# Sliding-window attention into a feed-forward layer: loads of the first blocks reordered and paired, the division of three blocks moved behind AV

## The chip, the cores and the metric

The kernel runs on one core of a Trainium2 chip. The metric is device microseconds of that core, the median of three runs. A profile is one execution, taken by the hardware profiler.

## The reference

```python
# q, k, v: (8, 8, 576, 64) f32; out: (4608, 512) f32
scores = q @ k.T / 8;  only |i - j| <= 32 is kept (others -1e9)
attn   = softmax(scores)                     # sum + 1e-9 below
x      = (attn @ v) as (4608 tokens, 512 = 8 heads x 64)
h      = x @ w_in                            # (512, 2048)
g      = s * relu(h)**2 + b                  # s, b: one number each
out    = g @ w_out                           # (2048, 512)
```

## The kernel before

The 4608 tokens are cut into 36 blocks of 128. For block j the attention needs 128 rows of q, and k and v from 32 rows before the block to 96 beyond, which lie in the tiles j and j+1 (k and v are loaded with an offset of 32 rows). The steps of one block are these:

- `load_k`, `load_q`, `load_v` (L456) put f32 tiles of 128 tokens into SBUF, by one DMA each (two where a tile spans two sequences). In HBM a token's 64 numbers of one head lie together: 256 bytes.
- `cast_k`, `cast_q`, `cast_v` make bf16 copies (`kqn`, `ve`); `make_vo` makes a second copy of v with its halves shifted (`vo`).
- `k_turn` (L546) and `q_turn` (L559) transpose k and q on TensorE for the first blocks (up to `KQDMA` = 8), with a copy out of PSUM (`kqt`); later blocks use a DMA transpose for k and q together (L539).
- `attend`: 16 or 24 small score matmuls (`sc`, L596), on VectorE the mask with the row minimum (L605), on ScalarE eight exponentials with row sums (L612, its accumulator is read by an extra instruction), on VectorE 1e-9 added and a reciprocal (L620, L623), then eight products p times 1/sum (L477; blocks 0 to 2 share them between ScalarE, VectorE and GpSimd, later blocks leave them to GpSimd), a transpose of p (TensorE for j below `PDMA` = 4, L646; else a DMA transpose, L639), AV matmuls (`av`, L667) and a copy into `xt` (bf16).

The feed-forward layer (FFN) works on tiles of 128 tokens (8 of them) and then 256 tokens (14). Its first layer (L758) multiplies `xt` by `win`, ScalarE takes the relu (L767), VectorE squares into `gt` (L786). The second layer (L809) accumulates 16 slices of `wout` in PSUM, four matmuls at a time; VectorE scales by s, adds `cvec` and writes `outs` (L818). `cvec` is b times the column sums of w_out, by matmuls of ones (L694) as the slices of w_out come in. The weights come in eight f32 DMAs of 1 MB (i0 to i3 for w_in, o0 to o3 for w_out; L431), staged in parts of `gt` that are not used yet, and are cast by three engines.

All work is listed first, as nodes with their reads, writes, an engine (or a choice of engines), a cost and a key. A planner (`order`) then simulates the five engines and SP's DMA ring and, on each engine, takes the ready node with the lowest key. The keys are token positions, shifted by kind of work through a table `RANK`. `akey(j)` gives attention's key, ahead of the FFN by up to `LEAD` tokens. TensorE nodes that use a part of its array have a mode other than 0; the planner charges a switch of modes and favours staying (`STICK`). Where it sees TensorE idle in the head, it puts in matmuls of ones that compute nothing (`fill`, L408). The loads are chained to each other on SP's queue; the first of them follow a written list:

```python
FIRST = "k0 k1 q0 v0 v1 k2 q1 v2 i0 i1 i2 k3 q2 v3 k4 q3 v4 i3 o0 o1 o2 o3|||"
PDMA, KQDMA, AHEAD, GATE = 4, 8, 4, 5
```

A `|` separates what is issued at the start from what is issued after block 0, 1, ... of attention has been listed. From then on, the loads of block j + `AHEAD` follow block j. The two scalars s and b (`scb`) are loaded on ScalarE's queue at the start.

Of the kernel before, what the change touches and what calls it, by code (L numbers as in the profile page):

```python
# [5 lines left out]
F32 = mybir.dt.float32  # L6
# [4 lines left out]
S = 576  # L11
# [12 lines left out]
START, RING, ISSUE, LAND, TURN = 800.0, 2400.0, 700.0, 2000.0, 600.0  # L24
PE_SLACK, STEADY = 400.0, 60000.0
SWITCH, STICK, STAY = 95.0, 1500, 60000.0
BIAS = {"act": 0.0, "dve": 400.0, "pool": 0.0}
FILL, FILL_MIN, FILL_SHARE, FILL_NS, WARM = ("attn", "ffn", "sums"), 300.0, 0.7, 115.0, 9000.0


class _Node:
# [4 lines left out]
                 "hard", "mode")  # L36

    def __init__(self, nid, eng, fn, cost, lat, key, dsem, ndma, dtime):
# [21 lines left out]
        self.mode = 0  # L60


class _Plan:
# [10 lines left out]
    def add(self, eng, fn, cost, key, reads=(), writes=(), dsem=None, ndma=1, dtime=0.0,  # L74
            after=(), behind=None, ndesc=128):
        n = _Node(len(self.nodes), eng, fn, cost, 300.0 if eng == "pe" else 130.0, key, dsem,
                  ndma, dtime)
        n.ndesc = ndesc

# [23 lines left out]
    def order(self):  # L103
# [14 lines left out]
        dma_free = {"sp": 0.0, "pool": 0.0, "act": 0.0}  # L118
# [14 lines left out]
        while len(out) < len(self.nodes):  # L133
# [29 lines left out]
            if e == "pe" and n.mode != mode:  # L163
                free[e], mode = free[e] + SWITCH, n.mode
            if n.dsem is None:
                end = free[e] + n.lat
            else:
                early = t < STEADY
                if e == "sp" and early:
                    free[e] = room(free[e], n.ndesc)  # L170
                dma_free[e] = max(dma_free[e], free[e] + (ISSUE if early else 1300.0)) + n.dtime
                if e == "sp" and early:
                    dma_free[e] += TURN if (n.ndesc == 512) != (kind == 512) else 0.0
                    kind = n.ndesc
                end = dma_free[e] + (LAND if early else 700.0)
                if e == "sp":
                    queue.append((dma_free[e], n.dtime, n.ndesc))
                    del queue[:-12]
            for u in n.users:
                if u.deps[n] is None:  # L180
                    u.ready = max(u.ready, free[e])
                else:
                    late = PE_SLACK if u.eng == "pe" and t > STEADY else 0.0
                    u.ready = max(u.ready,
                                  end + late if u.eng != n.eng or n.dsem else free[e] + 60.0)
                u.left -= 1
                if u.left == 0:
                    offer(u)
# [70 lines left out]
    stage = None  # L259


def bass_sliding_window_symmetric__then__act_starrelu_kernel(
# [15 lines left out]
    LEAD, L0, LS = 640, 300, 50  # L278
    RELU, SQ = 400, 200
    FIRST = "k0 k1 q0 v0 v1 k2 q1 v2 i0 i1 i2 k3 q2 v3 k4 q3 v4 i3 o0 o1 o2 o3|||"  # L280
# [3 lines left out]
    PDMA, KQDMA, AHEAD, GATE = 4, 8, 4, 5  # L284
# [5 lines left out]
    NSPLIT, NWHOLE, NSOLO = 0, 0, 0  # L290

    RANK = ({"ptc": 200, "ou": 120, "no": -20, "av": -120, "vo": 0, "ktc": 0, "ck": 200, "rc": -160, "cv": 20, "ktd": 320, "cq": 400, "wo": 340, "s1": -240, "kt": -60, "wi": -40, "xt": -280, "re": 80, "pt": -40}, {"vo": 40, "pt": -60, "ex": -200, "ck": -320, "s2": -80, "av": 580, "qt": -320, "mx": 320, "s1": -20, "sc": 40, "kt": 80})
    EARLY = 12

    def rank(kind, j):
        return RANK[0 if j < EARLY else 1].get(kind, 0)

# [15 lines left out]
    with ExitStack() as es:  # L313
# [10 lines left out]
        NL, NB, NVE, NVO, NKT, NP, NS, NPT, NG, NR1, NO, NM = 4, 4, 5, 4, 5, 4, 4, 3, 12, 4, 4, 4  # L324
# [4 lines left out]
        Q32 = [sb((128, DM), F32, "q32") for _ in range(NL)]  # L329
        K32 = [sb((128, DM), F32, "k32") for _ in range(NL + 1)]  # L330
# [18 lines left out]
        ONES = sb((128, 256), BF16, "ones")  # L349
        NIL = sb((128, 128), BF16, "nil")  # L350
# [8 lines left out]
        PTPF = ps((128, 512), F32, "ptp")  # L359
        AV = ps((128, NPAIR, 128), F32, "av")  # L360
# [13 lines left out]
        add("dve", lambda e: e.memset(NIL[:], 0.0), 100, K0, writes=["NIL"])  # L374
        add("dve", lambda e: e.memset(FLAT[:, 0, :], NEG), 100, K0, writes=[("FLAT", 0)])
        add("dve", lambda e: e.memset(FLAT[:, 1, :], 0.0), 100, K0, writes=[("FLAT", 1)])
        add("dve", lambda e: e.memset(K32[0][0:32, :], 0.0), 485, K0 + 10, writes=[("K32", 0, "lo")])
# [24 lines left out]
        def fill(e, stage, n):  # L402
            for _ in range(n):
# [3 lines left out]
                else:  # L407
# [8 lines left out]
        add("act", lambda e: [e.dma_start(SCB[:, 0:1], moe_s[0:1].partition_broadcast(128)),  # L416
                             e.dma_start(SCB[:, 1:2], moe_b[0:1].partition_broadcast(128))],
            900, K0, writes=["SCB"], dsem="dscb", ndma=2, dtime=400)
# [3 lines left out]
        wcnt = [0]  # L422

        def load_w(which, c):
            s_ = wcnt[0] % 4
# [4 lines left out]
                   else w_out[:, 4 * c:4 * c + 4, :])  # L430
            lastload[0] = add("sp", lambda e: [e.dma_start(w32, src)], 500, -LEAD - 900,  # L431
                              writes=[("W32", s_, g) for g in range(4)], dsem=f"dw{s_}",
                              dtime=2780, behind=lastload[0], ndesc=512)
# [18 lines left out]
        def load(src, t0, dst, name, key, sem, x):  # L452
            pcs = parts(t0)

            def fn(e):
                return [e.dma_start(dst[r:r + n, :].rearrange("p (h d) -> p h d", h=H),  # L456
                                    src[b, :, s0:s0 + n, :].rearrange("h s d -> s h d"))
                        for (b, s0, r, n) in pcs]

            tot = sum(n for (_, _, _, n) in pcs)  # L460
            gate = turned.get(x - GATE)
            lastload[0] = add("sp", fn, 640.0 * len(pcs), key, writes=[name], dsem=sem,
                              ndma=len(pcs), dtime=1150.0 * tot / 128, behind=lastload[0], ndesc=8 * tot,
                              after=[gate] if gate and gate.eng == "pe" else [])
# [3 lines left out]
        def cast(engs, src, sname, dst, dname, key, costs=None):  # L468
            move(engs, costs or {"act": 620.0, "dve": 425.0, "pool": 640.0}, dst, src, key,
                 sname if isinstance(sname, list) else [sname], [dname])  # L470

        def move(engs, costs, dst, src, key, reads, writes, scale=None):
# [12 lines left out]
            if isinstance(engs, str):  # L485
                return add(engs, fns[engs], costs[engs], key, reads=reads, writes=writes)
            return add(tuple(engs), fns, costs, key, reads=reads, writes=writes)

        def load_q(j):
            s_ = j % NL  # L490
            load(q, 128 * j, Q32[s_], ("Q32", s_), 128 * j - LEAD - 600, f"dq{s_}", j)

        def cast_q(j):
            s_, d_ = j % NL, (j + 1) % NB
# [3 lines left out]
        def load_k(j):  # L498
            s_ = j % (NL + 1)
            load(k, 128 * j - 32, K32[s_], ("K32", s_), 128 * j - LEAD - 730, f"dk{s_}", j - 1)  # L500

        def cast_k(j):
            s_, d_ = j % (NL + 1), j % NB
            cast(CSET(j), K32[s_][:, :], [("K32", s_)] + ([("K32", 0, "lo")] if j == 0 else []), KQN[d_][:, 0:DM],
# [12 lines left out]
        def make_vo(j):  # L517
# [9 lines left out]
            for r0, x in ((64, j), (0, j + 1)):  # L527
                sl = x % (NL + 1)
                move(OSET(j), {"act": 620.0, "dve": 425.0},
# [5 lines left out]
        def k_turn(j):  # L535
            kn, kt = j % NB, j % NKT
            key = akey(j) - 128
            if j > KQDMA:
                add("sp", lambda e: [e.dma_start_transpose(KQT[kt][:, :, :], KQN[kn][:, :])],  # L539
                    1300, key + 64 + rank("ktd", j), reads=[("KN", kn), ("QN", kn)],  # L540
                    writes=[("KT", kt), ("QT", kt)], dsem=f"dkt{kt}", dtime=1600, ndesc=1024)
# [8 lines left out]
            move(FLEX(j - 1), {"dve": 430.0, "act": 620.0}, KQT[kt][:, 0:NPAIR, :], TP[:, 0:4, :],  # L550
                 key + rank("ktc", j), ["TP"], [("KT", kt)])

        def q_turn(j):
            qn, qt = (j + 1) % NB, (j + 1) % NKT
            key = akey(j)

            def fn(e):
                for pr in range(NPAIR):
                    r = e.transpose(TP[:, 4 + pr, :],  # L559
                                    KQN[qn][:, DM + 128 * pr:DM + 128 * pr + 128], IDENT[:, :])  # L560
                return r

            if j >= KQDMA:
                return
            add("pe", fn, 240, key + rank("qt", j), reads=[("QN", qn), "IDENT"], writes=["TP"])
            move(FLEX(j), {"dve": 430.0, "act": 620.0}, KQT[qt][:, NPAIR:2 * NPAIR, :], TP[:, 4:8, :],
                 key + rank("qtc", j), ["TP"], [("QT", qt)])

        def attend(j):
# [7 lines left out]
            def half(blk, pr, a):  # L577
                return ((NKT - 1 - blk) * 2 * NPAIR + pr) * 2 + a

# [20 lines left out]
            add("pe", scores, 215, key + rank("sc", j), reads=[("KT", ka), ("KT", kb), ("QT", kb)],  # L600
# [284 lines left out]
```

## Time and profile before

| | |
|---|---|
| median of three runs | 322.82 us (322.29 to 323.59) |
| span of the profiled execution, first to last instruction | 322.6 us |
| TensorE busy | 309.6 us (96%), 3437 matmuls |
| ScalarE, VectorE, GpSimd busy | 237.1, 219.0, 188.1 us |
| HBM read, written | 36.70 MB, 9.44 MB |

No time is recorded for the profiled execution beside its span; the span lies within the three runs' range. Busy time of TensorE includes the matmuls of ones. A row of a timeline reads: start, duration (us), engine, line, operation, what it writes and reads, how many were merged, and in brackets the idle time before it with what ended it. A row of a table of windows reads: window, its length, then busy time and instruction count of PE, PEld, DVE, ACT and POOL, the granted clock, the busy share of the DMA engines and GB/s.

### The profile page before, as it was taken

The page shows a single profiled execution, that of the slowest core. Times are in us where ns is not written, and L with a number is a line of the kernel's source. Part 1 is how long each engine was busy: PE and PEld are TensorE (multiplying, and loading weights), DVE is VectorE, ACT ScalarE, POOL GpSimd, SP SyncE. Part 2 cuts the span into 40 slices and gives each one's busy share as a digit, 9 for nine tenths or more (in the row PEclk, how much of TensorE's full clock was granted, in tenths as well). Part 3 has the DMA queues.
Part 4 walks back from the last instruction along what each step waited for, and adds up shares of the span by engine and source line. Part 5 has one row for each costly group of instructions (what it writes and reads, how often), then busy time and mean ns, then how long its engine had stood idle before and what let it go on. Part 6 is the DMA issues. An engine that isn't in the chain of part 4 may idle for free.

```text
span 322.6 us, 9452 instructions
## 1 busy us (share of the span) xinstructions
PE 309.6 (96%) x3437; PEld 210.7 (65%) x3437; DVE 219.0 (68%) x939; ACT 237.1 (73%) x804; POOL 188.1 (58%) x402
## 2 busy tenths in 40 slices
PE   6879899998999999999999999999999999999996
PEld 4557675757775766566666766676766666766664
DVE  3657848976896678787677875678776766644242
ACT  4988977896995878797578986788889888624130
POOL 1555785886878275769565887467686754420000
PEclk9999999999999999999999999999999999999999
DMA  7999999999999999999999999999999992230011
GB/s 143 293 285 267 399 262 221 213 207 216 201 215 182 257 212 178 223 212 227 214 217 219 200 197 216 216 230 188 194 234 211 240 157 67 68 98 2 33 68 65
DMA packets 185887, 62.49 MB, mean 194 GB/s; under 512 B 177008, under 2 KB 177264, under 8 KB 185840
## 3 DMA queue, kind: packets, MB, share of 16 engines
q1 hardware_dynamic: 185552, 61.88, 94.6%
q8 instruction: 27, 0.44, 0.6%
q14 instruction: 20, 0.16, 0.2%
q10 hardware_dynamic: 288, 0.00, 0.0%
HBM read 36.70 MB, written 9.44 MB: 143 GB/s over the span
## 4 chain that ended last, share of the span: by engine, by line
PE 77%; SPq 8%; DMA 8%; POOL 3%; DVE 2%; ACT 1%; issue 1%; POOLq 0%
PE ht L758 24%; PE outp L809 15%; PE ptp L809 15%; PE tp L758 10%; SPq L456 7%; PE av L667 4%; DMA q<-in_q_dram 3%; PE sc L596 3%; PE sc L809 2%; DMA kqt<-kqn 2%; POOL p L477 2%; DMA v<-in_v_dram 2%; PE av L809 2%; DMA pts<-p 1%; PE outp L694 1%; SPq L431 1%
## 5 line engine op out<-in xcount | busy, mean ns | idle before, releaser
L477 POOL TENSOR_SCALAR p<-p,rc 128x128 bf16<-128x128 bf16 x275 | 112.7, 428 | 35.9 <-DVE rc L623 35.9
L612 ACT ACTIVATE p<-ss,mx 128x128 bf16<-128x128 f32 x288 | 111.8, 391 | 11.1 <-DVE mx L605 10.6
L758 PE MATMUL ht<-xt,win 128*128 128x256 bf16 (+1 forms) x1104 | 106.5, 248 | 0.2
L786 DVE TENSOR_TENSOR gt<-r 128x512 bf16<-128x512 bf16 x144 | 71.3, 497 | 48.2 <-ACT r L767 46.3
L758 PEld LDWEIGHTS ht<-xt,win 128*128 128x128 bf16 x1104 | 86.5, 98 | 18.2 <-ACT r L767 0.6
L767 ACT ACTIVATE r<-ht 128x512 bf16<-128x512 f32 x106 | 62.4, 591 | 31.2 <-PE ht L758 29.7
L605 DVE CUSTOM_DVE_ANT_0 ss<-sc,mask 128x128 f32<-128x128 f32 x288 | 66.2, 282 | 8.8 <-PE sc L596 8.5
L809 PE MATMUL outp<-wout,gt 128*128 128x512 bf16 (+1 forms) x272 | 67.8, 373 | 0.0
L809 PE MATMUL ptp<-wout,gt 128*128 128x512 bf16 x256 | 65.5, 379 | 0.0
L612 ACT ACTIVATION_READ_ACCUMULATOR p<-ss,mx 128x1 f32 x288 | 54.6, 189 | 0.0
L758 PE MATMUL tp<-xt,win 128*128 128x256 bf16 x304 | 39.4, 273 | 0.0
L809 PEld LDWEIGHTS ptp<-wout,gt 128*128 128x128 bf16 x256 | 24.2, 98 | 22.1
L809 PEld LDWEIGHTS outp<-wout,gt 128*128 128x128 bf16 x272 | 24.9, 98 | 20.1
L476 POOL CAST ve<-v 128x512 bf16<-128x512 f32 x37 | 24.1, 651 | 24.0 <-PE av L667 14.4
L481 ACT CAST vo<-v 64x512 bf16<-64x512 f32 x45 | 27.6, 614 | 12.0 <-PE av L667 10.3
L758 PEld LDWEIGHTS tp<-xt,win 128*128 128x128 bf16 x304 | 29.3, 98 | 7.5
L476 POOL CAST kqn<-k 128x512 bf16<-128x512 f32 x33 | 21.4, 648 | 20.8 <-DMA k<-in_k_dram 20.7
L767 ACT ACTIVATE r<-tp 128x512 bf16<-128x512 f32 x38 | 22.4, 590 | 14.6 <-PE tp L758 13.3
L476 DVE CAST xt<-av 128x512 bf16<-128x512 f32 (+1 forms) x34 | 23.1, 680 | 9.0 <-PE av L667 8.8
L476 POOL CAST kqn<-q 128x512 bf16<-128x512 f32 x34 | 22.5, 661 | 10.4 <-DMA q<-in_q_dram 10.3
L605 DVE DVE_READ_ACCUMULATOR2_ANT mx<- 128x1 f32 x288 | 23.0, 80 | 0.0
L596 PEld LDWEIGHTS sc<-kqt 64*64 64x64 bf16 x632 | 9.8, 106 | 12.5 <-issue 8.5
(69 smaller groups left out, 229.7 us busy)
## 6 DMA issues: line engine op xcount, KB each, us to landing
out_dram<-outs SPq DMA_DIRECT2D x35, 256.0 KB, 2.9
q<-in_q_dram SPq DMA_DIRECT2D x32, 256.0 KB, 4.7
k<-in_k_dram SPq DMA_DIRECT2D x28, 256.0 KB, 4.5
v<-in_v_dram SPq DMA_DIRECT2D x28, 256.0 KB, 4.8
gt<-in_moe_w_in_dram SPq DMA_DIRECT2D x4, 1024.0 KB, 8.3
gt<-in_moe_w_out_dram SPq DMA_DIRECT2D x4, 1024.0 KB, 9.3
k<-in_k_dram SPq DMA_DIRECT2D x8, 192.0 KB, 3.6
v<-in_v_dram SPq DMA_DIRECT2D x8, 192.0 KB, 4.3
```

The lines of the kernel that those rows point to most:

```text
L456: return [e.dma_start(dst[r:r + n, :].rearrange("p (h d) -> p h d", h=H), src[b, :, s0:s0 + n, :].rearrange("h s d -> s h d")) for (b, s0, ...
L476: return e.tensor_copy(dst, src)
L477: return e.tensor_scalar(dst, src, scale, 1.0, ALU.mult, ALU.mult)
L481: return e.copy(dst, src)
L596: r = e.matmul(dst, rhs=rhs, start=True, stop=True, lhsT=KQT[kb][r0:r0 + 64, NPAIR + pr, 64 * u:64 * u + 64])
L605: lambda e, ss=ss, x=x, y=y: e.tensor_tensor_reduce(out=SS[ss][:, x, :], in0=SC[y % 2][:, y // 2, :], in1=MASK[kind][:, :], scale=-SCALE, ...
L612: lambda e, ss=ss, x=x, y=y: e.activation(P[pb][:, y, :], SS[ss][:, x, :], AF.Exp, bias=MX[mb][:, y:y + 1], scale=-1.0, accum_out=SM[mb][: ...
L667: r = e.matmul(avp[64 * hh:64 * hh + 64, pr, 64 * u:64 * u + 64], lhsT=vt[k0:k1, 128 * pr + 64 * hh:128 * pr + 64 * hh + 64], rhs=PTS[ptb] ...
L758: r = e.matmul(hbank[:, nt * f:nt * f + nt], lhsT=WIN[:, kc, 128 * ft:128 * ft + 128], rhs=XT[:, kc, x0:x0 + nt], start=(kc == 0), stop=(k ...
L767: return e.activation(R1[rb][:, :], hbank[:, :], AF.Relu, bias=0.0, scale=1.0)
L786: return e.tensor_tensor(d, r, r, ALU.mult)
L809: r = e.matmul(op_[:, 0:cn], lhsT=GT[:, g_, fc, :], rhs=WOUT[:, fc, c0:c0 + cn], start=(fc == 0), stop=(fc == 15))
```

## The change

- The list of first loads is new. k and q of the first ten blocks come in pairs of blocks: `K0` is the k of blocks 0 and 1, and so on. One partition takes two neighbouring tokens, so that a run in HBM is 512 bytes. Tokens of four blocks come before the first weight; w_in is loaded in one piece, then v4 and K2, then w_out and, last, the scalars, now on SP's queue.
- The pairs are cast in two strided halves and turned together (`turn_pair`); the copy out of PSUM puts even and odd tokens back in order with a stride. `KQDMA` goes from 8 to 10, so k 9, k 10, q 8 and q 9 are turned on TensorE too.
- Blocks 0 to 2 (`NPN`) no longer multiply p by 1/sum: the exponentials take no row sums, matmuls of ones give the sums in `xt`'s layout (with 1e-9 from a constant tile `EPS`), VectorE takes the reciprocal (`RB`) and multiplies where it copied AV into `xt`.
- Blocks 0 and 1 (`NSPLIT`) do without `vo`: their AV takes three steps on `ve` of two tiles.
- `AHEAD` goes from 4 to 3, `LEAD` from 640 to 512. `RANK` has a value for each kind and block. The planner's costs are new, as are `STICK` and the cost of a switch.
- Code for other settings (weights cast by DMA, AV and scores in one group: `WCAST`, `GRP`) comes in, and is not used with the values given: `WCAST` is empty and `GRP` is 99.

```diff
-FIRST = "k0 k1 q0 v0 v1 k2 q1 v2 i0 i1 i2 k3 q2 v3 k4 q3 v4 i3 o0 o1 o2 o3|||"
-PDMA, KQDMA, AHEAD, GATE = 4, 8, 4, 5
-NSPLIT, NWHOLE, NSOLO = 0, 0, 0
+PDMA, KQDMA, AHEAD, GATE, PAIR = 4, 10, 3, 5, 1950.0
+NPN, NSPLIT = 3, 2
+FIRST = "K0 Q0 v0 v1 K1 v2 Q1 v3 i0 i1 i2 i3|v4 K2 o0 o1 o2 o3 s0||"
+LEAD, L0, LS = 512, 300, 50
...
+        def load_pair(what, J):
...
+                return [e.dma_start(
+                    big[r:r + n // 2, 2 * DM * a:2 * DM * a + 2 * DM].rearrange("p (h x) -> p h x", h=H),
+                    src[b, :, s0:s0 + n, :].rearrange("h (p i) d -> p h (i d)", i=2)) for (b, s0, r, n) in pcs]
...
+        def turn_pair(what, J):
...
+                first = move(
+                    ("act", "dve"), {"dve": 560.0, "act": 530.0},
+                     KQT[kt][:, g0:g0 + NPAIR, :].rearrange("p g (t i) -> p g t i", i=2),
+                     bank[:, :, 64 * x:64 * x + 64].rearrange("p (i g) t -> p g t i", i=2),
...
+                if late:
+                    add("act", lambda e, ss=ss, x=x, y=y: e.activation(
+                        P[pb][:, y, :], SS[ss][:, x, :], AF.Exp, bias=MX[mb][:, y:y + 1], scale=-1.0),
...
+                if late:
...
+                    def sums(e, c0=c0, c1=c1, p0=p0, p1=p1):
+                        for hh in range(2):
+                            e.matmul(TPF[64 * hh:64 * hh + 64, 128 * p0:128 * p1], lhsT=ONES[:, 0:64],
+                                     rhs=EPS[:, 128 * p0:128 * p1], start=True, stop=False)
+                        for y in range(c0, c1):
+                            r0 = 64 * (y % 2)
+                            r = e.matmul(tot[r0:r0 + 64, y // 2, :], lhsT=ONES[:, 0:64],
+                                         rhs=PTS[ptb][:, y, :], start=False, stop=(y >= c1 - 2))
...
+                    add("dve", lambda e, p0=p0, p1=p1: e.reciprocal(
+                        RB[:, 128 * p0:128 * p1], TPF[:, 128 * p0:128 * p1]), 60 + 135 * (p1 - p0),
...
+                    add("dve", lambda e, p0=p0, p1=p1, avp=avp: e.tensor_tensor(
+                        XT[:, p0:p1, 128 * (j % NX):128 * (j % NX) + 128], avp[:, p0:p1, :],
+                        RB[:, :].rearrange("p (a b) -> p a b", b=128)[:, p0:p1, :], ALU.mult),
```

## The prediction

> **What bounds the kernel now.** I read the page's slices first, then TensorE's own timeline, then a table of short windows for the DMA, then SP's and GpSimd's timelines at the places that the chain of waits names.
>
> The page's slices: each digit is eight microseconds.
>
> ```profile
> PE   6879899998999999999999999999999999999996
> PEclk9999999999999999999999999999999999999999
> ```
>
> TensorE is full from slice 6 on, at full clock. Its digits in the first 45 us flatter it: the view of groups by line has 113 matmuls of ones (L408), which compute nothing.
>
> ```profile
> L408 PE MATMUL ht<-ones 128*128 128x256 bf16 x76 | 12.3, 312 | 1.3 <-DVE nil L374 1.3
> L408 PE MATMUL outp<-ones 128*128 128x256 bf16 x37 | 5.7, 274 | 0.0
> ```
>
> The first 18 took 4.0 us; the others start about 0.11 us apart, so all of them fill some 14 us. The windows below give 8.2 us of idle TensorE up to 47.5 us. With some 2.8 us of short gaps the head loses 25 us; by 47.6 us, when the last `cvec` group ends, only 22.6 us of needed work is done. TensorE's timeline has the points that matter:
>
> ```profile
> 14.30 0.42 PE L596 MATMUL sc<-kqt 64*64 64x128 bf16 x16 [0.20 <-DVE kqt L476]
> 20.48 1.07 PE L758 MATMUL ht<-xt,win 128*128 128x128 bf16 x16
> 27.55 0.42 PE L596 MATMUL sc<-kqt 64*64 64x128 bf16 x16
> 46.72 1.03 PE L694 MATMUL outp<-wout,ones 128*128 128x512 bf16 x4
> 50.71 0.45 PE L596 MATMUL sc<-kqt 64*64 64x128 bf16 x24
> 65.71 0.32 PE L667 MATMUL av<-pts,ve 128*64 128x64 bf16 x8
> 68.27 1.95 PE L758 MATMUL ht<-xt,win 128*128 128x128 bf16 x32
> 71.78 0.32 PE L667 MATMUL av<-pts,ve 128*64 128x64 bf16 x8 [0.69 <-DMA pts<-p]
> 77.61 0.42 PE L596 MATMUL sc<-kqt 64*64 64x128 bf16 x16 [0.84 <-DMA kqt<-kqn]
> 132.36 0.32 PE L667 MATMUL av<-pts,ve 128*64 128x64 bf16 x8 [0.54 <-DMA pts<-p]
> ```
>
> The scores of blocks 1 and 2 stand 13 us apart, because k and q of block 2 come in behind three weight loads. The scores of block 4 come at 50.71, their AV at 65.71, the first FFN matmuls of block 4 (I call their start T) at 68.27. After 47.6 us only the last three rows wait, 2.1 us in all. So the kernel is a lossy head of 25 us and a TensorE-bound rest, and what the head is made of is the stream of loads:
>
> ```profile
> 10.00:12.50 2.50, 2.32 (x33) 1.59 (x33) 2.15 (x18) 2.21 (x7) 1.06 (x2) 1.00 1.14 232
> 15.00:17.50 2.50, 2.03 (x19) 1.60 (x19) 2.31 (x20) 1.93 (x9) 1.23 (x3) 1.00 1.04 404
> 22.50:25.00 2.50, 1.44 (x26) 1.07 (x24) 2.06 (x6) 2.11 (x6) 2.08 (x3) 1.00 0.69 157
> 42.50:45.00 2.50, 2.50 (x37) 2.03 (x35) 1.43 (x5) 2.07 (x5) 2.50 (x6) 1.00 1.16 234
> ```
>
> The last column is GB/s: about 215 while runs of 256 B (k, q, v) move, about 395 while weights (2 KB runs) move, and a dip to 157 where the stream changes from weights to tokens. In SP's timeline the dip has its cause, a load that could not be issued for six microseconds behind the weights; the later two rows are for the path of block 4 below:
>
> ```profile
> 12.81 5.94 SPq L456 DMA_DIRECT2D q<-in_q_dram  x1
> 57.69 2.51 SPq L456 DMA_DIRECT2D v<-in_v_dram  x2
> 60.24 2.44 SPq L639 DMA_TRANSPOSE pts<-p  x1
> ```
>
> **The stream of loads.** Before, up to the last w_out: k, q, v 3.54 MB at 215 is 16.5 us, weights 8.39 MB at 395 is 21.2, and a start of 2.9 (ramp) gives 40.6. The windows show the weights ending near 42.8 (a 2.5 us window at 234 is 0.3 us of 395 and the rest of 215), so the dip cost 2.2. After: K0, Q0, K1, Q1 and K2 are 2.56 MB in runs of 512 B, v0 to v4 1.25 MB at 215 (5.8 us), weights 21.2, start 2.9. The trace has no 512 B run. A line through the two rates (16 engines: 19 ns for 256 B, 83 ns for 2 KB) gives 28 ns, 290 GB/s, hence 8.8 us and an end at 38.7. The bounds are 215 (41.8) and 395 (36.4). I take 290, as the row at 256 B is the near one and the line starts from it. The dip I count as gone, since only v4 and K2 stand between the weight groups; if it stays, add 2.2. So w_out is complete 4.1 us earlier.
>
> The Trainium skill (DMA: Bandwidth & Descriptors, Specifications) says that transfers from 512 B on run at line rate. The slow 256 B rows agree with the other half of that rule. By it the pairs take the weights' 395, and the sum would be 2.8 us lower than mine: this is the first rival.
>
> **Block 4, which decides T.** Before, the last w_out slice was cast at 44.4, q4 at 46.4, scores 50.7. After, w_out is there at 40.3 and the Q2 pair (0.52 MB, 1.8 us) at 42.1; K2 came earlier, so only q must still be turned, and I take 3.4 us in place of 4.3: scores at 45.5. From scores to T it was 17.6 us. Of these, exps and sums took 4.5, GpSimd's eight products 2.8 (55.26 to 58.08), and then the turned p had to wait 2.2 us for SP, stuck in the v load above. With loads in pairs SP has fewer instructions ahead; I take 16.0, so T is 61.5. Bounds: 12.5 (each step at its own row: 4.5, 2.8, 3.9 for a pts transpose to land, 1.3 for AV and xt) and 17.6.
>
> What TensorE can do ahead of T is fixed: the FFN of blocks 0 to 3, `cvec`, and attention, 68.3 - 25.0 = 43.3 us. The loss up to T becomes 61.5 - 43.3 = 18.2, against 25.0: **6.8 us gained**. That blocks 0 to 3 come 10 us earlier on their own matters only as cover for this. It is enough: with w_in whole near 27 us, 14.2 us of first-layer and 3.4 us of `cvec` work reach to about 41, then 13.8 of second layer to about 55. What is left of the loss is about 13 us until then and 5 of waiting for block 4.
>
> **Division behind AV, blocks 0 to 2.** Removed: 24 products (428 ns on GpSimd, some on ScalarE and VectorE), 24 accumulator reads (about 0.09 us each beyond the overlap), 6 small sums and reciprocals. Added per half block: two 256-wide and four 128-wide matmuls of ones, about 0.45 us, 2.7 in all, inside the 14 us that fillers take now: nothing, or 2.7 if TensorE had no slack there. The six 128x256 reciprocals have no row: by the 0.42 us of a 128x256 PSUM cast on VectorE 2.5 us in all; by the slope from 128x4 (0.18) to 128x8 (0.20), 5 ns a column, 8.6. The low one is the nearer in shape. VectorE is idle over a third of 10 to 45 us, so both are hidden; uncovered they would push blocks 0 to 2 only. Eight strided k/q copies (0.42 now; at most the 0.75 of f32 rows) add up to 2.6 us there, and leaving out four vo casts gives back 2. The scalars move from ACT's queue to the end of SP's; they land about with the last w_out, ahead of `cvec`'s end. Zero; 1 us on one PSUM bank if late. The wider memset (0.5 more) lies in VectorE's idle 2 us before 5.8.
>
> **Turns of blocks 8 to 10 go from DMA to TensorE:** k 9 and 10, q 8 and 9, about 0.22 each, **+0.9** on the full engine. It takes away two 5.1 us transposes and with them the wait of 0.84 at 77.6. Of the 2.1 us of late waits I take **1.0** as gained; bounds 2.1 and -2 (AHEAD is 3 in place of 4).
>
> **Priorities.** Each attention step that stands between FFN groups costs about 0.1 us on entry (96.04 follows a group that ends at 95.93). 20 of the 72 steps stand beside another now. I take seven more: **0.7 gained**; bounds 0 and 2.8.
>
> Sum: 6.8 + 1.0 + 0.7 - 0.9 = 7.6. The span is 322.6, within 0.2 of the median 322.82 of three runs; 322.6 - 7.6 = **315.0**.
>
> **The clock.** PEclk is full in every slice, with the longest idle stretch of TensorE 1.39 us. If the 5 us of waiting for block 4 lie in one piece, no row here tells what the clock does. The Trainium skill (TensorE: Matmul & The Clock Gate, What's actually happening) says an idle window of about 3.4 us halves it until a busy window has passed: 1.7 us by that page, and the sum would be 316.7. My sum goes without it, because fillers and spread-out groups have kept every gap short so far.
>
> **Rivals.**
> - *Pairs at the weights' rate, and a smooth path of block 4*: 2.8 us less by the stream alone, **312**, and with the path's low bound of 12.5 about 309. For it: the weight rows at 395. Against: 512 B is nearer to 256 than to 2 KB. 0.18.
> - *The stream is no shorter* (it does not do what it says): pairs at 215 (+3.1) and the dip still there (+2.2) make T 66.8, **320**; the order of loads is fixed by a chain, so the order itself is sure. 0.12, and 0.06 that it ends within the noise, near 322.
> - *Slower: the lead in the steady stage is lost.* Loads go out one block later (AHEAD 3) and attention's keys are 512 tokens ahead in place of 640, so scores or AV of blocks 8 to 35 wait for DMA. Price: 0.69 a wait, the mean of the three rows. There are 56 such steps. It decides from 11 waits on (7.6 / 0.69); with 20, 13.8 us, **329**. Against it: the loads of before end near 258 us, 60 us ahead of the end. 0.09.
>
> **How the numbers follow.** Forecast case 0.55, with its own range 311 to 318 (T from 58 to 64). The range 308 to 321 takes in both first rivals and leaves out the slower one, most of the no-change case, and a little below: under 0.2. A measurement tells about 0.5% from no change, 1.6 us, so faster is below 321.2: 0.55 + 0.18 + 0.12 = 0.85; same 0.06; slower 0.09.
>
> **What would show it.** Right: scores of blocks 0 to 3 within one unbroken stretch before 30 us, w_out's last cast near 40, scores of block 4 near 45.5, T near 61.5, fewer L408 rows, a TensorE gap of some microseconds ahead of T. Wrong: T at 66 or later; a tail of `<-DMA pts` and `<-DMA kqt` waits past 100 us; or T far ahead of 58, where my path of block 4 is too long.

## The result, and the profile after

The changed kernel takes 324.65 us (median of 20 runs, 324.10 to 326.21), the kernel before 323.65 us beside it (20 runs, 322.29 to 325.18). The ratio is 1.0038, 95% interval 1.0023 to 1.0054: slower by 0.4%, where 315.0 against 322.82 (0.976) was forecast. The profiled execution after has a span of 323.1 us; before, 322.6. Medians of the kernel before lie between 323.65 and 324.88 us in the comparisons of this study, so below I go by ratios and by spans.

The slices of the page after, eight microseconds each:

```profile
PE   7787799989999999999999999999999999999996
PEclk9969999999999999999999999999999999999999
```

From slice 6 on TensorE is as full as before. The head is no fuller (7 7 8 7 7 against 6 8 7 9 8), and in the third slice the clock's digit is 6 where it was 9. The view of waits says what TensorE stood still for (waiting step, what it waited for; total us, times, longest):

```profile
PE tp L844 <- DVE rb L854: 3.4, 4, 1.3
PE av L825 <- DVE xt L857: 1.3, 1, 1.3
PE av L1011 <- DVE gt L987: 1.1, 1, 1.1
PE tp L605 <- DVE rb L854: 0.9, 1, 0.9
```

`rb` is the reciprocal of the late division. The matmuls of ones (L844) and a turn of k (L605) wait for it because both write the PSUM bank `tp`, and the AV at L825 waits for the product with `rb`: 5.6 us of idle TensorE in all. The view of one tile gives the duration (min/median/max in ns, first and last start):

```profile
L854 DVE RECIPROCAL rb<-tp x6: 1741/1750/1758, 13.5 to 33.6; 128x256 f32<-128x256 f32 x6
```

So 1.75 us each, 10.5 us in all; the prediction had 0.42 and 2.5, with 8.6 as the upper bound. TensorE's timeline after, for the points that were shown of before:

```profile
8.65 0.42 PE L727 MATMUL sc<-kqt 64*64 64x128 bf16 x16
15.36 0.43 PE L844 MATMUL tp<-eps,ones 128*64 128x256 bf16 x2 [0.86 <-DVE rb L854]
17.86 1.03 PE L605 MATMUL tp<-ident,kqn 128*128 128x128 bf16 x8 [0.89 <-DVE rb L854]
20.10 0.64 PE L727 MATMUL sc<-kqt 64*64 64x128 bf16 x16
22.79 0.42 PE L727 MATMUL sc<-kqt 64*64 64x128 bf16 x16
23.37 1.06 PE L959 MATMUL ht<-xt,win 128*128 128x128 bf16 x16
39.12 0.42 PE L727 MATMUL sc<-kqt 64*64 64x128 bf16 x16
53.16 0.45 PE L727 MATMUL sc<-kqt 64*64 64x128 bf16 x24
71.88 1.95 PE L959 MATMUL ht<-xt,win 128*128 128x128 bf16 x32
131.13 1.04 PE L1011 MATMUL outp<-wout,gt 128*128 128x512 bf16 x4 [0.19 <-DVE gt L987]
```

Scores of block 1 stand at 20.10 (14.30 before), of block 3 at 39.12, of block 4 at 53.16 (forecast 45.5), and T, the first FFN of block 4, at 71.88 (68.27 before, forecast 61.5). The first FFN matmuls come at 23.37 (20.48). After T only 0.19 us of waiting is left, where before had 2.1. From T to the end it is 251.2 us (254.3 before). The table of windows (same columns as before: after the five engines the granted clock, the busy share of the DMA engines, GB/s) shows the clock, the pairs (first two rows) and the dip (last row):

```profile
5.00:7.50 2.50, 1.53 (x19) 0.96 (x17) 0.69 (x1) 1.58 (x3) 1.07 (x2) 1.00 1.30 245
7.50:10.00 2.50, 2.37 (x39) 1.86 (x38) 0.88 (x9) 1.72 (x4) 1.23 (x2) 1.00 1.22 267
15.00:17.50 2.50, 1.61 (x14) 1.13 (x14) 2.19 (x3) 0.77 (x2) 0.29 (x1) 0.50 1.06 407
17.50:20.00 2.50, 2.14 (x14) 1.59 (x14) 1.15 (x3) 1.16 (x4) 1.20 (x3) 0.50 1.05 401
25.00:27.50 2.50, 1.15 (x18) 0.78 (x16) 2.50 (x7) 1.58 (x5) 0.61 (x3) 1.00 1.25 222
```

### The profile page after: what moved, and what is told of

Same layout as the page of the kernel before. It is cut to its first block, busy times and chain, and to the rows that moved or that the text cites. A ratio compares the mean times of both kernels' runs of the same rounds, so it can differ in the third digit from the quotient of the medians.

```text
span 323.1 us, 9454 instructions
## 1 busy us (share of the span) xinstructions
PE 309.8 (96%) x3462; PEld 211.9 (66%) x3462; DVE 213.9 (66%) x911; ACT 236.7 (73%) x785; POOL 177.1 (55%) x396
## 4 chain that ended last, share of the span: by engine, by line
PE 88%; DVE 7%; ACT 2%; DMA 1%; issue 0%
PE ht L959 28%; PE av L1011 19%; PE outp L1011 18%; PE tp L959 10%; PE av L825 4%; PE sc L727 4%; DVE rb L854 3%; PE sc L1011 2%; DVE ss L755 2%; PE tp L605 1%; DMA k<-in_k_dram 1%; DVE gt L987 1%; PE outp L877 1%; PE ht L452 1%; ACT p L762 1%; DVE win L544 1%
## 5 line engine op out<-in xcount | busy, mean ns | idle before, releaser
L545 POOL TENSOR_SCALAR p<-p,rc 128x128 bf16<-128x128 bf16 x264 | 103.6, 412 | 80.4 <-DVE rc L779 80.4
L768 ACT ACTIVATE p<-ss,mx 128x128 bf16<-128x128 f32 x264 | 102.8, 391 | 5.6 <-DVE mx L755 5.1
L959 PEld LDWEIGHTS ht<-xt,win 128*128 128x128 bf16 x1128 | 88.9, 98 | 13.1 <-issue 0.4
L987 DVE TENSOR_TENSOR gt<-r 128x512 bf16<-128x512 bf16 x144 | 67.6, 472 | 36.9 <-ACT r L968 35.6
L1011 PE MATMUL av<-wout,gt 128*128 128x512 bf16 (+1 forms) x288 | 68.0, 374 | 1.1 <-DVE gt L987 1.1
L1011 PE MATMUL outp<-wout,gt 128*128 128x512 bf16 (+1 forms) x272 | 61.8, 373 | 0.2 <-DVE gt L987 0.2
L549 ACT CAST vo<-v 64x512 bf16<-64x512 f32 x50 | 30.8, 616 | 27.0 <-PE av L825 26.0
L768 ACT ACTIVATION_READ_ACCUMULATOR p<-ss,mx 128x1 f32 x264 | 50.3, 191 | 0.0
L1011 PEld LDWEIGHTS av<-wout,gt 128*128 128x128 bf16 x288 | 26.7, 98 | 29.0 <-DVE gt L987 1.3
L544 DVE CAST xt<-av 128x512 bf16<-128x512 f32 x33 | 22.8, 690 | 19.2 <-PE av L825 18.2
L755 DVE DVE_READ_ACCUMULATOR2_ANT mx<- 128x1 f32 x288 | 23.3, 81 | 0.0
L1020 DVE SCALAR_TENSOR_TENSOR outs<-outp,scb,cvec 128x512 f32<-128x512 f32 (+1 forms) x17 | 12.4, 730 | 15.8 <-PE outp L1011 15.7
## 6 DMA issues: line engine op xcount, KB each, us to landing
gt<-in_moe_w_in_dram SPq DMA_DIRECT2D x4, 1024.0 KB, 10.4
```

What stands on the lines that cost most here:

```text
L544: return e.tensor_copy(dst, src)
L545: return e.tensor_scalar(dst, src, scale, 1.0, ALU.mult, ALU.mult)
L549: return e.copy(dst, src)
L755: lambda e, ss=ss, x=x, y=y: e.tensor_tensor_reduce(out=SS[ss][:, x, :], in0=SC[y % 2][:, y // 2, :], in1=MASK[kind][:, :], scale=-SCALE, ...
L768: lambda e, ss=ss, x=x, y=y: e.activation(P[pb][:, y, :], SS[ss][:, x, :], AF.Exp, bias=MX[mb][:, y:y + 1], scale=-1.0, accum_out=SM[mb][: ...
L959: r = e.matmul(hbank[:, nt * f:nt * f + nt], lhsT=WIN[:, kc, 128 * ft:128 * ft + 128], rhs=XT[:, kc, x0:x0 + nt], start=(kc == 0), stop=(k ...
```

## The experiments

Two theories after this result. *A*: the reciprocals set the time; they stand in VectorE's queue and hold the bank that the sums and turns need. *B*: something else that the change moved, with the reciprocals beside it: the order in which the planner lists the work, the loads, or block 4's path. Some expectations add *C* (the half clock between 15 and 22 us is the loss) or *D* (a new order, and not the new instructions, costs the time). In the kernels called "order kept", the instructions of every engine stand as in the changed kernel; in the others the planner puts all in order anew.

**The reciprocals as copies, order kept.** The division of blocks 0 to 2 is left out of what is computed.

```diff
-                    add("dve", lambda e, p0=p0, p1=p1: e.reciprocal(
+                    add("dve", lambda e, p0=p0, p1=p1: e.tensor_copy(
```

> The six reciprocals of the late division are replaced by plain copies of the same shape, nothing else: the division of blocks 0 to 2 is left out, and every engine keeps its instruction order. Theory A (the reciprocals): L854 holds 10.1 us of the chain's first 75 us at 1.75 us each; as copies of about 0.42 us it can give back at most 7.6 us, so 316 to 319 us. Theory B (the order of loads: k of block 4, which block 3 needs, lies behind w_in, so that something else is late anyway): 323 to 325. Theory C (the half clock between 15 and 22 us is the loss, whatever stands before it): 320 to 322 if the clock stays full now, 324 if it drops again.

Measured: 319.88 us, ratio 0.985 (0.980 to 0.989), span 318.9, clock 1.0 throughout, T at 67.7. The same tile in the same place, at 0.42 us, is worth 4.2 us of span. A stands, but it leaves 3.9 us of span above the 315.0 forecast.

**Each reciprocal twice, order kept** (the first result goes to a tile that nobody reads).

```diff
+                        e.reciprocal(EXTRA[:, 128 * p0:128 * p1], TPF[:, 128 * p0:128 * p1])
                         return e.reciprocal(RB[:, 128 * p0:128 * p1], TPF[:, 128 * p0:128 * p1])
```

> Each of the six reciprocals is done twice (the first result goes to a tile that nothing reads); order of all engines kept. 10.5 us more on VectorE. Theory A (one for one on the path of blocks 0 to 2, five or six of them in series): 332 to 335. Theory C (it is the clock, which is already at half there): 325 to 328.

Measured: 336.68 us, ratio 1.038 (1.034 to 1.042), span 334.5, clock 0.969, T at 83.3. Some ten microseconds more of reciprocals (six of 1.75 us; the second of each two takes 1.69) make the span 11.4 longer, all of it ahead of T. Its waits:

```profile
PE tp L845 <- DVE rb L857: 8.6, 4, 2.9
PE tp L606 <- DVE rb L857: 2.5, 1, 2.5
PE av L826 <- DVE xt L861: 2.0, 1, 2.0
```

13.1 us in place of 5.6. What is added to the 1.75 us is not hidden any more: the price is one for one, and a little above it, with a lower clock (0.969 against 0.989). Below 1.75 us it is another matter: the copies take 8.0 us less of VectorE's time (six times 1.33) and give back 4.2, so about half of what the reciprocals take beyond a copy was hidden.

**1/sum as exp(-ln(sum)) on ScalarE, the planner free to put all in order anew.**

```diff
-                    add("dve", lambda e, p0=p0, p1=p1: e.reciprocal(
+                    add("act", lambda e, p0=p0, p1=p1: e.activation(RB[...], TPF[...], AF.Ln, bias=0.0, scale=1.0), 300,
...
+                    add("act", lambda e, p0=p0, p1=p1: e.activation(RB[...], RB[...], AF.Exp, bias=0.0, scale=-1.0), 300,
```

> 1/sum as exp(-ln(sum)) on ScalarE, two activations of 128x256 in place of each reciprocal on VectorE; the planner orders anew. The result is whole. Theory A: two activations of about 0.35 us each in place of 1.75 us: 317 to 320. Theory B: 323 to 325.

Measured: 327.40 us, ratio 1.008 (1.004 to 1.012), span 326.6, T at 71.25. The slow instruction is gone, and the kernel is slower. Either the work itself, or its new order, costs more; the next kernel tells which.

**The same two activations, order kept.** The planner still sees the reciprocal; once the order stands, its node becomes the logarithm and a node for the exponential is put right behind it. `RB` has two buffers.

```diff
-        order = self.order()
+        order = []
+        for n in self.order():
+            order.append(n)
+            if n.swap is None:
+                continue
+            m = _Node(len(self.nodes), "act", n.swap[1], 300.0, 120.0, n.key, None, 1, 0.0)
...
+            n.eng, n.fn, m.deps = "act", n.swap[0], {n: True}
...
+            order.append(m)
```

> 1/sum as exp(-ln(sum)) on ScalarE, as in the run with two activations that came out at 327.4, but the planner's order is kept: every engine runs the changed kernel's sequence, only the six reciprocals are gone from VectorE and twelve activations stand at their places in ScalarE's. Result whole. Theory A (each reciprocal's length counts): 319 to 321, near the 319.9 of the plain copies. Theory D (the 327.4 came from the new order, not from the activations) says the same; if the activations themselves are the trouble, it stays at 326 to 328.

Measured: **319.73 us** (319.56 to 320.32), ratio 0.986 (0.983 to 0.989), span 318.6, T at 67.4. It computes the whole reference and beats both kernels, by 1.4% the one before and by 1.8% the changed one (0.9859 / 1.0038). The tile's rows show what took the reciprocal's place:

```profile
L870 ACT ACTIVATE rb<-tp x6: 373/378/383, 14.2 to 29.1; 128x256 f32<-128x256 f32 x6
L872 ACT ACTIVATE rb<-rb x6: 416/416/417, 14.7 to 29.5; 128x256 f32<-128x256 f32 x6
```

0.79 us in place of 1.75, on an engine that is not the full one, and the bank is free after 0.38. No wait for `rb` is left in TensorE's list. Against the run above, which has the same instructions (and one buffer of `RB`; with one buffer and the order kept, the copies took 319.88), the order is worth 7.7 us. The keys and ranks of the change fit one plan; a cost that is nearer to the truth makes another plan, and a worse one.

**The planner told the reciprocal's true cost** (1.75 us in place of 0.33; `RB` doubled, order anew).

```diff
-                        RB[:, 128 * p0:128 * p1], TPF[:, 128 * p0:128 * p1]), 60 + 135 * (p1 - p0),
+                        RB[:, 128 * p0:128 * p1], TPF[:, 128 * p0:128 * p1]), 60 + 845 * (p1 - p0),
```

> The reciprocals stay, but the planner is given their measured price (1.75 us for 256 columns in place of 0.33), with a second buffer for their results. Theory A in its form that the planner's wrong price made the order bad: 318 to 321. Theory A in its form that 10.5 us of VectorE on the path of blocks 0 to 2 cost time in any order: 321 to 324. Theory B: 323 to 325.

Measured: 337.11 us, ratio 1.038 (1.033 to 1.042), span 335.5: 12 us worse than with the wrong cost. **No late division at all** (order anew):

```diff
-NPN, NSPLIT = 3, 2
+NPN, NSPLIT = 0, 2
```

> The late division is undone (NPN 0): blocks 0 to 2 take row sums with the exponentials and multiply p by 1/sum before the transpose, as before the change; the rest of the change stays, and the planner orders anew. Theory A: 24 products and 24 accumulator reads come back, 10.5 us of reciprocals go: 317 to 321. Theory B: 324 to 327, since the late division would have been a help.

Measured: 334.52 us, ratio 1.031 (1.026 to 1.036), span 332.4. T comes at 71.68, 0.2 us earlier than in the changed kernel, but from there to the end it takes 260.7 us in place of 251.2. One of the places, in its timeline:

```profile
292.10 1.33 PE L1011 MATMUL sc<-wout,gt 128*128 128x512 bf16 x3 [3.52 <-DVE mx L755]
```

Attention of the last blocks stands unfinished near the end, and TensorE waits 3.5 us for a mask. The kernel with the true cost has the same wait at 295.18. So neither run says what the late division alone is worth; both say that this plan does not survive a new order.

**More matmuls of ones in the reciprocal's shadow, order kept**: eight ahead of the second sums of block 0, eight ahead of K1's turn.

```diff
+            if n.more:
+                n.pre = ("attn", n.more + (n.pre[1] if n.pre else 0))
```

> Reciprocals and order as in the changed kernel; 16 more matmuls of ones, eight ahead of the second sums of block 0 and eight ahead of the second turn of blocks 2 and 3, where TensorE waited 0.9 us each for a reciprocal and its clock fell to half. Theory C: with the clock full, about 2 us come back (the chain holds some 4 us of matmuls at half speed between 15 and 22 us): 322 to 323. Theory A: the chain waits for VectorE, not for TensorE's clock: 324 to 325.

Measured: 323.49 us, ratio 0.997 (0.995 to 0.999), span 322.5, and the clock is full from 12.5 to 25 us. It then falls to half from 26.8 to 30.2 us, behind a wait of 1.31 us for a reciprocal that was 1.31 us long in the changed kernel too and had no drop behind it there:

```profile
15.00:17.50 2.50, 2.50 (x30) 1.93 (x28) 2.41 (x3) 1.10 (x2) 0.54 (x1) 1.00 1.06 409
17.50:20.00 2.50, 2.05 (x35) 1.43 (x34) 1.52 (x4) 1.22 (x3) 0.92 (x2) 1.00 1.04 399
27.50:30.00 2.50, 2.44 (x29) 2.04 (x28) 2.33 (x3) 1.66 (x4) 1.65 (x4) 0.50 0.93 243
```

Against the changed kernel it gains 0.6 us by the spans of the profiled executions, 1.2 by the medians of all spans (321.75 against 322.95) and 2.1 (1.3 to 3.0) by the ratios. Of its ten executions, six have a mean clock of 0.999 or 1.0 and spans of 321.0 to 321.8; the other four, the profiled one among them, have 0.989 or 0.995 and 321.9 to 322.7; the changed kernel has 0.989 or less in all twenty. So work that computes nothing makes the kernel faster, through the clock, but it doesn't keep the clock full in every execution. The slower clock is the smaller part of what the reciprocals cost.

**Each pair loaded by two DMAs in runs of 256 bytes** (with the two activations, order kept).

```diff
-                    big[r:r + n // 2, 2 * DM * a:2 * DM * a + 2 * DM].rearrange("p (h x) -> p h x", h=H),
-                    src[b, :, s0:s0 + n, :].rearrange("h (p i) d -> p h (i d)", i=2)) for (b, s0, r, n) in pcs]
+                    big[...].rearrange("p (h i d) -> p i h d", h=H, i=2)[:, i, :, :],
+                    src[b, :, s0:s0 + n, :].rearrange("h (p i) d -> p i h d", i=2)[:, i, :, :])
+                    for (b, s0, r, n) in pcs for i in range(2)]
```

> As the run with twelve activations at the reciprocals' places, order kept, but each pair load goes as two DMAs of 256-byte runs in place of one of 512-byte runs, into the same places. Against that run: if the stream of loads sets the head and pairs move at 290 GB/s in place of 215, 2 to 3 us slower; if something else sets it, no difference beyond 1 us.

Measured: 324.80 us, ratio 1.001 (0.997 to 1.004), span 324.5, so 5 us slower than with pairs (the spans of the profiled executions differ by 5.9). Two windows of it, at 219 and 217 GB/s; with pairs they have 245 and 261:

```profile
5.00:7.50 2.50, 1.66 (x17) 1.03 (x15) 0.46 (x1) 1.20 (x2) 0.61 (x1) 1.00 1.32 219
7.50:10.00 2.50, 1.64 (x30) 1.23 (x31) 0.24 (x1) 1.69 (x3) 1.67 (x3) 1.00 1.35 217
```

Block 4's scores come at 50.97 in place of 48.62, 2.4 us later. The rest arises later: block 4's AV waits 1.89 us for its transpose, and right behind that TensorE runs at half clock (0.50 granted from 70 to 72.5 us). A group of four second-layer matmuls shows it; elsewhere such a group takes 1.03 us:

```profile
69.79 1.77 PE L1029 MATMUL av<-wout,gt 128*128 128x512 bf16 x4
```

**Half of every w_out load left out, and with it half of w_out** (two activations, order kept).

```diff
-            lastload[0] = add("sp", lambda e: [e.dma_start(w32, src)], 500,
+            lastload[0] = add("sp", lambda e: [e.dma_start(w32, src) if which == "i" else e.dma_start(w32[:, 0:2, :], src[:, 0:2, :])], 500,
```

> From the run with exp(-ln(sum)) in kept order (319.7): each of the four w_out loads brings only half of its rows (0.5 MB in place of 1 MB; half of w_out is left out), everything else and all orders kept. If the stream of loads up to w_out sets T (the first FFN matmuls of block 4, 67.5 us there) and T sets the end: the last cvec group comes 3 to 5 us earlier, T 62.5 to 64.5, and the time is 315 to 317. If the path from the scores of block 4 to T has its own limit: 318.5 to 320.

Measured: 319.39 us, ratio 0.985 (0.981 to 0.989), span 317.8, T at 66.5. Two megabytes less in the stream gain 0.9 us of T, 0.8 of span and 0.3 of the median: the end of the stream is not what sets T. The last `cvec` group comes 0.8 us earlier (44.19 in place of 45.03) and not 3 to 5, since its last casts now start without a wait for the load, at 42.30, but behind a relu on ScalarE. The 0.76 us that TensorE had waited there for a cast is gone, and that is about what T gained.

**Block 4's eight products on 8 of 128 columns** (the rest of its p stays undivided; two activations, order kept).

```diff
-                         P[pb][:, y, :], P[pb][:, y, :], key - 300 + rank("no", j),
+                         P[pb][:, y, 0:(8 if j == 4 else 128)], P[pb][:, y, 0:(8 if j == 4 else 128)],
+                         key - 300 + rank("no", j),
```

> From the same run: the eight products of p by 1/sum of block 4 on GpSimd cover 8 columns of 128 (the division of block 4 is left out for the rest), orders kept. If the steps of block 4 from its scores to T are the limit, T moves by most of the 2.8 us that the products take: 317 to 318. If T is held by the fixed order of VectorE (squares of block 3 stand behind the eight mask operations of block 6) and of TensorE: 319 to 320, T unchanged.

Measured: 320.05 us, ratio 0.988 (0.984 to 0.991), span 318.1, T at 66.84. The experiment is weaker than meant: on 8 columns the eight products still take 2.75 us, against 3.42, so the path became only 0.7 us shorter. T is 0.54 earlier, but not through the products: block 4's scores, which lie ahead of them, are already 0.77 earlier (47.85), with 0.22 us in place of 0.76 of waiting for the last cast of w_out. Its own timeline says more. The products end at 56.15, block 4's AV starts at 63.93 with no wait ahead of it, and the one wait of TensorE after 45 us is for a square of the FFN:

```profile
62.97 1.04 PE L1029 MATMUL av<-wout,gt 128*128 128x512 bf16 x4 [1.36 <-DVE gt L1005]
```

In the kernel with full products it is the same: AV of block 4 at 64.47, without a wait. Block 4's path has slack here; TensorE comes to it late.

**K2 and v4 ahead of the weights** (two activations, order anew).

```diff
-FIRST = "K0 Q0 v0 v1 K1 v2 Q1 v3 i0 i1 i2 i3|v4 K2 o0 o1 o2 o3 s0||"
+FIRST = "K0 Q0 v0 v1 K1 v2 Q1 v3|K2 v4 i0 i1 i2 i3 o0 o1 o2 o3 s0||"
```

> exp(-ln(sum)) on ScalarE with the planner ordering anew, as in the run that came out at 327.4, but K2 and v4 are loaded ahead of the weights (FIRST: ... Q1 v3|K2 v4 i0 i1 i2 i3 o0 ...). Block 3 needs the k tiles 3 and 4, and tile 4 is in K2: if that holds its scores back (34.1 us in the run with kept order, 37.3 in the one at 327.4; 33.8 before the change), they come at 25 to 29 now. The time itself also has the new order in it: 324 to 330, so only the scores of block 3 tell.

Measured: 325.43 us, ratio 1.002 (0.998 to 1.006), span 324.6: 2 us better than the other kernel with activations in a new order, T at 68.57 against 71.25. Block 3's scores were to come early and did not: K2 is cast from 17.6 us on, but its turn is left until

```profile
34.29 0.61 PE L605 MATMUL tp<-ident,kqn 128*128 128x128 bf16 x8
```

and the scores follow at 36.94. The new order puts that turn behind block 2's division, though its data lay there for 16 us; and w_in, now last, lets the first FFN start only at 24.86. This run therefore doesn't show what an early block 3 would be worth.

## Why the prediction was wrong, point by point

**The frame held.** T was to set the gain and the rest to be full. After, from T to the end it is 251.2 us in the changed kernel and also, within 0.1 us, with the copies, with the activations in the kept order, with the doubled reciprocals and with more matmuls of ones. Whatever moves T in the kept order moves the end. The forecast span was 315.0 with T at 61.5, so 253.5 behind T. It became 323.1: 10.4 us more in T, 2.3 less behind it.

**The term that decided the sign: "so both are hidden".** The late division's reciprocals were given 0.42 us by a cast of the same shape, "nearer in shape"; they take 1.75, above even the bound by the slope (1.43 each). The copy in the first experiment, on the same tile, takes 0.42: the shape alone does not give the duration. The Trainium skill (VectorE: DVE Perf Modes, First, the fixed hardware budget) says that the reciprocal is an iterative divide with a repeat count of 8; it is not put as a duration there; the two rows, 1.75 against 0.42, agree in direction, with a factor of 4.2. The second half of the step, that they would lie in idle time of VectorE, failed as well. "Idle over a third of 10 to 45 us" was itself misread: the row of that window before has VectorE (third of the engines) busy for 25.15 of 35 us, so 9.9 us or 28% idle, less than the 10.5 us of reciprocals.

```profile
10.00:45.00 35.00, 30.14 (x433) 23.09 (x434) 25.15 (x117) 31.13 (x106) 22.93 (x40) 1.00 1.04 316
```

And idle time of an engine covers work only if nobody waits for that work. Here the sums of the next half block and the turns of K1 and K2 need the one bank `tp` (the turns of Q0 and Q1 have another, `ht`), so block 0's two reciprocals and K1's turn behind them stand in series. Doubled, the reciprocals cost 11.4 us; replaced, they give back 4.5 (323.1 to 318.6). "Uncovered they would push blocks 0 to 2 only" missed that block 1's scores stand behind K1's turn, and the FFN behind them.

**The clock.** The prediction looked for a drop at the wait for block 4 and left it out. It came at 14.8 to 21.6 us, at half clock, although no idle stretch just ahead of it or in it is above 0.9 us and before had one of 1.39 without a drop. "Fillers have kept every gap short so far" no longer held in the same way: the changed kernel has 70 matmuls of ones, before had 113. The Trainium skill (TensorE: Matmul & The Clock Gate, What's actually happening) ties the drop to an idle window of about 3.4 us; no idle stretch of that length is in this trace. Filling two of the gaps kept the clock there, at 0.6 to 2.1 us gained, but in the profiled execution half clock came later, from 26.8 to 30.2 us, behind a gap of 1.31 us. So the length of a gap alone does not decide here. What exactly is counted, these runs don't tell.

**The rest of the miss: what TensorE has done by when.** With the reciprocals out of the way T is 67.4, still 5.9 us late. The prediction let 17.6 us of FFN and `cvec` work be done by about 41 us, lost 13 us of TensorE's time up to then, and had it wait 5 us for block 4. Counted from the groups by line in windows from 0, at 0.216 us for 512 columns, the work done is this:

| FFN and `cvec` done by | 30 us | 40 us | 50 us | 60 us |
|---|---|---|---|---|
| before | 3.5 | 7.3 | 16.8 | 23.5 |
| changed | 1.7 | 6.6 | 16.0 | 23.3 |
| activations, order kept | 3.3 | 11.7 | 19.0 | 26.8 |

By 30 us none of the three has done more than 3.5, where the prediction's 17.6 us by 41 need 6.6 by then. From 30 us to T the kernel with the activations has about 2.1 us of idle TensorE and no wait for block 4, so T is 30 plus the 27.8 us of FFN work that is left and the attention between. This fits that a shorter stream hardly moves T, and that block 4's AV has no wait ahead of it. From block 4's scores to T it takes 18.8 us there (18.7 in the changed kernel), where 16.0 was taken with 17.6 as the upper bound: not block 4's own steps fill it, but TensorE's other work. The step "with w_in whole near 27 us, 14.2 us of first-layer and 3.4 us of `cvec` work reach to about 41" took for granted that blocks 0 to 3 were through attention by then. In the kernel with the activations `xt` of block 1 is whole at 27.45 us and that of block 2 at 31.15, and the last casts of w_in end at 29.2, after a wait for the load:

```profile
27.03 0.42 DVE L874 TENSOR_TENSOR xt<-av,rb 128x256 bf16<-128x256 f32 x1 [0.33 <-ACT win L562]
30.73 0.42 DVE L874 TENSOR_TENSOR xt<-av,rb 128x256 bf16<-128x256 f32 x1 [0.70 <-PE av L838]
27.55 1.65 POOL L557 CAST win<-gt 128x512 bf16<-128x512 f32 x2 [2.85 <-DMA gt<-in_moe_w_in_dram]
```

And block 3's keys are partly in K2, which lies behind w_in. GpSimd's timeline of that kernel has its cast, and the wait for the load:

```profile
31.92 0.71 POOL L557 CAST kqn<-k 128x512 bf16<-128x512 f32 x1 [2.17 <-DMA k<-in_k_dram]
```

Block 3's scores follow at 34.10, no earlier than before (33.82). "Tokens of four blocks come before the first weight" holds for three blocks, as far as TensorE is concerned, and the forecast of scores of blocks 0 to 3 "within one unbroken stretch before 30 us" could have been seen to fail from `FIRST` alone. No run changed one of these three alone, so how much of the 5.9 us each accounts for stays open.

**The loads.** Pairs were put at 290 GB/s (bounds 215 and 395). Windows that mix pairs and v have 245 to 293, and taking the pairs away made block 4's scores 2.4 us later, against 3.1 worked out between 215 and 290. This term was about right: in half-microsecond windows of the changed kernel, 286 to 293 GB/s stand where, by the bytes moved up to then, Q0 and K1 move (5.0 to 5.5 and 8.5 to 9.0 us), and no more than 347 for the first pair (3 to 4 us). "The dip I count as gone" was not: v4 and K2 still pull a window to 222 GB/s, and the stream ends near 40.7 in place of 38.7, by an estimate (the window from 40 to 42.5 has 115 GB/s, 0.7 us of 400). With the activations ScalarE waits for the last slice of w_out until 43.3, where 40.3 was forecast. Part of this was a misreading: 44.4 is where VectorE's last cast of w_out starts before, but GpSimd's last two end at 46.4, and 4.1 us ahead of that is 42.3:

```profile
44.96 1.43 POOL L476 CAST wout<-gt 128x512 bf16<-128x512 f32 x2
```

With T set elsewhere, that cost little. The first rival (pairs at the weights' rate) is out. Of the rival "the stream is no shorter" the pairs at 215 did not come about; the dip stayed. The end of the stream at w_out holds under 1 us of the 5.9, as the halved w_out loads show.

**Behind T.** The rival of the lost lead is out: no wait for a DMA after T, with one block less in advance. The gain of 3.1 us has 1.9 from late waits that went (2.07 to 0.19; I took 1.0) and 0.9 from the last second-layer work of blocks 0 to 3, which now lies ahead of T (by T 13.8 us of second layer, before 13.0). The 0.3 left over holds priorities and turns together, taken as 0.7 gained and 0.9 lost.

So the span is 8.1 us above the forecast: 10.4 late in T, less 2.3 behind T. Of the 10.4, 4.5 are the reciprocals (with the clock), shown by replacing them in the kept order. The other 5.9 are the difference that is left; that they stand for work which TensorE could not start before 30 us is read from the timelines, and no run has taken them away.

## What to carry to other kernels

Price an operation by a row of that operation; the duration of a copy of the same shape is no stand-in, and where no row exists, the upper bound belongs into the forecast with its whole chain, the buffer that it holds included. "Hidden on an idle engine" needs two questions: how much the engine is idle in that stretch, and who waits for the result or for the bank. Where a planner's costs and ranks were fitted together, test one part with the order kept: here the same instructions took 319.7 us in the old order and 327.4 in a new one, and a truer cost made it 337.1.

## What the runs showed of the hardware that was not expected

- A reciprocal of 128x256 f32 from PSUM on VectorE takes 1.75 us, a copy 0.42; ln and exp on ScalarE take 0.38 and 0.42.
- TensorE's clock fell to half in a stretch whose longest gap is 0.9 us (14.8 to 21.6 us, changed kernel). Sixteen more matmuls that compute nothing kept it full there and made the kernel 0.6 to 2.1 us faster; in the profiled execution it fell later, from 26.8 to 30.2 us, behind a gap of 1.31 us that the changed kernel has without a drop.
